# Combine weights turned by VectorE and DMAs instead of TensorE, in the second expert mixture

## The chip, the cores and the metric

The kernel runs on one core of one Trainium2 chip, as one launch. The metric is the time of that launch on the device in microseconds. The core has TensorE (matmuls, with a weight load PEld that overlaps them), VectorE (DVE), ScalarE (ACT), GpSimd (POOL) and SyncE (SP), whose queue issues the DMAs.

## The reference

Three stages follow one another: an attention with a memory, a soft mixture of experts, and a second mixture whose weights are balanced by eight rounds of normalisation. The change touches only the third.

```python
def _moe_ref(x, phi, w1, w2):
    ...
    c = logits - logits.max(1, keepdims=True)
    c = np.exp(c)
    c /= c.sum(1, keepdims=True) + 1e-09
    return (c @ slot_out).astype(np.float32)      # [2304, 32] @ [32, 512]

def _moe2_ref(x, w_gate, w1, w2):                 # N = 2304, D = 512, E = 8, F = 1024
    logits = x @ w_gate
    logits = logits - logits.max()
    P = np.exp(logits)
    for _ in range(8):
        P /= P.sum(1, keepdims=True) + 1e-09
        P /= P.sum(0, keepdims=True) + 1e-09
        P *= N / E
    out = np.zeros((N, D), dtype=np.float32)
    for e in range(E):
        h = np.maximum(x @ w1[e], 0.0)
        ye = h @ w2[e]
        out += P[:, e:e + 1] * ye
    return out.astype(np.float32)
```

## The kernel before, in words

The input x of the second mixture is c @ slot_out, with only 32 slots. So the kernel doesn't form x. For each expert it multiplies the 32 slot rows with w1 once (`prepare_a`, line 1092, the slots' product `pa`), splits the result into a high and a low part (`split_a`) and spreads both by DMAs into a tile `a4` of 128 rows (`move_a`, line 1125). The first layer is then `layer1` (line 1145): a matmul of `a4` with `c4T`, which holds c transposed, 128 rows by 2304 tokens: two copies of the rounded c and two of its remainder, 32 rows each. The product of the four row blocks gives the full precision. As relu commutes with a positive factor, the expert's weight P[:, e] is folded into c. So `c4T` must be made anew for each expert.

Making it (lines 1313 to 1338) is done in pieces of two units by three steps. `scale_c`: VectorE multiplies c by the weight (`cP`), ScalarE rounds it (`chi`) and writes it twice into `c4`, VectorE writes the remainder twice. `turn_c`: TensorE transposes each tile of 128 tokens into PSUM (`pc`, line 1331). `store_c`: ScalarE copies the result to `c4T` (line 1336). Pieces of an expert come at units 6 to 9 and, for the last unit's two tiles (the leftovers), at unit 10, counted from the start of the expert before; `c_steps` puts the three steps behind products 1, 2 and 3 of the unit.

The work is cut into units: 8 experts by 9 units of 256 tokens. A unit's second layer is a product of 2 x 2 blocks in seven block products (`PRODS`, in the `ORDER` p5, p1, p7, p6, p2, p3, p4), numbered k = 0 to 6. Each is 12 matmuls of 128 x 256: over four row blocks f, high by high (line 1451), high by low (1452), low by high (1453). After product 1 of unit g comes `layer1` of unit g + 1, eight matmuls. So a unit is 84 + 8 = 92 matmuls. The first five units of expert 0 use a plain product instead.

Around the products, `hidden` makes the seven left operands of the next unit from PSUM: ScalarE rounds (line 1175) and VectorE (1169, 1182) and GpSimd (1186) make sums and remainders. `collect` adds finished products into the accumulators (1467). The weights of the next expert are summed and split by `w_sum` (1045), `w_hi` (1048, ScalarE) and `w_lo` (1054, GpSimd, one of them VectorE) in the same way. The late blocks B11, T3, B21 and B22 (tiles `BB1`, `BB2`) are shared by all experts, so they are rounded only in the last unit of the expert before and the first of the new one, just behind their last use.

The order is written out by hand: `beside(s, f, ...)` appends a step to slot s = 7 g + k, `at(u, k, ...)` is slot 7 u + k, and in each slot the program emits the product, then `hidden` and `collect`, then what `beside` left there. Each engine runs its own instructions in that order; they wait for each other by semaphores. SP issues its DMAs in the same program order but runs ahead of the other engines until one of its own waits stops it: the loads of w1 and w2 wait for the tiles' last readers, `move_a` for `split_a`. The buffer `ps_a` in PSUM, one bank, serves `pc` and `pa` in turn.

One earlier DMA is of use below: `load_memory` (line 174) moves, in the first stage, 64 partitions x 4 pairs of heads x 65 numbers of 4 bytes.

Of the kernel before, what the change touches and what calls it, by code (L numbers as in the profile page):

```python
# [8 lines left out]
F32 = mybir.dt.float32  # L9
# [12 lines left out]
def infini_attention_soft_moe_sinkhorn_moe(  # L22
# [22 lines left out]
    P = 128  # L45
# [1006 lines left out]
    def w_lo(e, nm, i, g):  # L1052
# [9 lines left out]
    Cw = mD.tile([P, NTT, NS], F32, name="Cw")  # L1062
    sel = mD.tile([P, 4, 160], F32R, name="sel")
    nc.vector.tensor_scalar(
        out=sel.rearrange("p j c -> p (j c)"), in0=ones[:, 0:1].to_broadcast([P, 640]),
        scalar1=0.0, scalar2=None, op0=ALU.mult,
# [157 lines left out]
    m2 = mS.tile([1, 1], F32, name="m2")  # L1224

    def gate_slots():
        soB = G["soB"] = mB.tile([P, KD, 4, NS], F32, tag="c4", name="soB")
        nc.scalar.activation(out=soB, in_=soR.to_broadcast([P, KD, 4, NS]), func=AF.Copy)
# [84 lines left out]
    def scale_c(e, u0, u1):  # L1313
        T0, n = 2 * u0, 2 * (u1 - u0)
        cP = mB.tile([P, 4, NS], F32, tag="cP", name="cP")[:, 0:n]
        nc.vector.tensor_tensor(
            out=cP, in0=Cw[:, T0 : T0 + n], in1=Pr[:, T0 : T0 + n, e : e + 1].to_broadcast([P, n, NS]),
            op=ALU.mult,
        )
        chi = mB.tile([P, 4, NS], F32R, tag="chi", name="chi")[:, 0:n]  # L1320
        nc.scalar.activation(out=chi, in_=cP, func=AF.Copy)
        c4 = cs_[e, u0] = mB.tile([P, 4, 4, NS], F32, tag="c4", name="c4")
        hb = chi.bitcast(F32).rearrange("p t (o s) -> p t o s", o=1).to_broadcast([P, n, 2, NS])
        cb = cP.rearrange("p t (o s) -> p t o s", o=1).to_broadcast([P, n, 2, NS])
        nc.scalar.activation(out=c4[:, 0:n, 0:2, :], in_=hb, func=AF.Copy)
        nc.vector.tensor_tensor(out=c4[:, 0:n, 2:4, :], in0=cb, in1=hb, op=ALU.subtract)
# [8 lines left out]
    def store_c(e, u0, u1):  # L1335
        nc.scalar.activation(
            out=c4T[:, UT * u0 : UT * u1], in_=G["pc"][:, 0 : UT * (u1 - u0)], func=AF.Copy
        )


    side = {}
# [27 lines left out]

    def c_steps(v, e, u0, u1):  # L1370
        at(v, 1, scale_c, e, u0, u1)
        at(v, 2, turn_c, e, u0, u1)
        at(v, 3, store_c, e, u0, u1)

# [14 lines left out]
    for e in range(1, E):  # L1389
        v = NU * (e - 1)  # L1390
        for i in range(5):
            c_steps(v + 6 + i, e, 2 * i, min(2 * i + 2, NU))
        at(v, 0, load_w1, e, e % 2)
# [3 lines left out]
        at(v + 1, 4 + (e == 1), split_a, e)  # L1397
        at(v + 1, 5 + (e == 1), move_a, e)
        for i in range(2):
# [6 lines left out]
            at(v + 6 + i, 2, w_sum, e, "T3", i, "P")  # L1406
        for nm, k in (("B11", 2), ("T3", 4), ("B21", 6), ("B22", 8)):
            for i in range(2):
                at(v + 8, k + i, w_hi, e, nm, i)
                at(v + 8, k + i + (nm[0] == "B" and nm[1] == "2"), w_lo, e, nm, i, "D" if nm == "B22" and i else "P")  # L1410
# [30 lines left out]
    def product(g, k):  # L1441
        e, u = units[g]
        a, b = PRODS[ORDER[k]]
        bank, half = PLACE[ORDER[k]]
        if (g, bank) not in Y:
            Y[g, bank] = ps_y.tile([P, DM], F32, tag="y", name=bank)
        o_ = Y[g, bank][:, CW * half : CW * half + CW]
        hh, hl = X[g, a, "h"], X[g, a, "l"]
        wh, wl = W[e, b, "h"], W[e, b, "l"]
        for f in range(KH):  # L1450
            nc.tensor.matmul(o_, hh[:, f, :], wh[:, f, :], start=f == 0, stop=False)  # L1451
            nc.tensor.matmul(o_, hh[:, f, :], wl[:, f, :], start=False, stop=False)  # L1452
            nc.tensor.matmul(o_, hl[:, f, :], wh[:, f, :], start=False, stop=f == KH - 1)  # L1453
        return o_
# [197 lines left out]
```

## Time and profile before

| | us |
|---|---|
| median of 3 runs | 1119.05 |
| the runs | 1119.82, 1119.05, 1113.94 |
| the profiled execution | 1122.88 |
| its span | 1120.9 |

The second mixture fills the profile from about 300 us to the end. TensorE is busy for 97% of the span, so a time is best read from the distance between the starts of its instructions, not from their durations: a 128x256 matmul is shown with 0.28 us, and the next one starts 0.11 us later. DVE is busy for 74%, POOL for 63%, ACT for 58%.

### The profile page before, as it was taken

The numbers are of one execution on the slowest core, as the hardware profiler recorded it, in microseconds if no ns is written. First come the engines' busy times: TensorE is split into PE (matmuls) and PEld (weight loads), VectorE is DVE, ScalarE is ACT, GpSimd is POOL, SyncE is SP. The second block draws the span as 40 slices with busy tenths as digits, with TensorE's granted clock in tenths as the row PEclk, the third lists the DMA queues.
The fourth block names the chain that finished last, engine by engine and source line by source line (L and its number), as shares of the span: only waits on it lengthen the run. The fifth ranks groups of instructions, "written<-read, shape, count | busy, mean of one in ns | idle before, by whom it ended". The sixth has DMA issues, their size and how long they took to land.

```text
span 1120.9 us, 24593 instructions
## 1 busy us (share of the span) xinstructions
PE 1085.3 (97%) x9269; PEld 996.0 (89%) x9269; DVE 830.7 (74%) x1813; ACT 645.4 (58%) x1392; POOL 703.7 (63%) x634
## 2 busy tenths in 40 slices
PE   6999999989999999999999999999999999999998
PEld 4887878763577899999999999999999999999998
DVE  7888888753266467788778778877977777788775
ACT  7988989741343675556455545644564555456442
POOL 6655556300252777688577768866776676778665
PEclk8999999988899999999999999999999999999999
DMA  9476767578702013004101300310030022000111
GB/s 208 127 215 188 222 183 216 152 290 346 313 22 73 1 54 107 12 1 142 29 1 39 118 16 1 113 58 1 11 142 20 1 102 69 1 2 20 44 53 58
DMA packets 42646, 105.73 MB, mean 94 GB/s; under 512 B 8224, under 2 KB 18592, under 8 KB 38432
## 3 DMA queue, kind: packets, MB, share of 16 engines
q1 hardware_dynamic: 42096, 104.07, 28.6%
q8 instruction: 74, 1.21, 0.4%
q14 instruction: 44, 0.36, 0.1%
q10 hardware_dynamic: 432, 0.09, 0.0%
HBM read 95.74 MB, written 4.72 MB: 90 GB/s over the span
## 4 chain that ended last, share of the span: by engine, by line
PE 80%; DVE 6%; ACT 5%; DMA 4%; issue 4%; POOL 1%; SPq 0%; DVEq 0%; ACTq 0%; POOLq 0%
PE y L1451 19%; PE y L1452 19%; PE y L1453 19%; PE l L1145 6%; PE po L476 3%; PE pt L437 2%; ACT sm L394 2%; PE y L1418 2%; DMA wm<-in_moe_w_dram 2%; PE pa L1092 1%; PE pc L1331 1%; DMA w<-in_moe_w_dram 1%; PE ps L371 1%; PE ps L366 1%; DVE sm L387 1%
## 5 line engine op out<-in xcount | busy, mean ns | idle before, releaser
L1169 DVE SCALAR_TENSOR_TENSOR f<-l,f 128x512 f32<-128x512 f32 x268 | 184.2, 687 | 59.7 <-ACT a11h L1175 49.8
L1186 POOL TENSOR_TENSOR s1l<-f,s1h 128x512 fp32r<-128x512 f32 x67 | 90.3, 1347 | 155.2 <-ACT s1h L1175 155.2
L1467 DVE TENSOR_TENSOR accA<-accA,y 128x512 f32<-128x512 f32 x125 | 85.5, 684 | 48.6 <-PE y L1453 48.3
L1175 ACT ACTIVATE a12h<-l 128x512 fp32r<-128x512 f32 x72 | 43.2, 600 | 101.8 <-PE y L1453 95.0
L1186 POOL TENSOR_TENSOR s4l<-f,s4h 128x512 fp32r<-128x512 f32 x67 | 87.4, 1304 | 15.7 <-PE y L1452 10.3
L1467 DVE TENSOR_TENSOR accB<-accB,y 128x512 f32<-128x512 f32 x125 | 85.7, 686 | 7.5
L1186 POOL TENSOR_TENSOR s3l<-f,s3h 128x512 fp32r<-128x512 f32 x67 | 87.1, 1299 | 0.0
L1186 POOL TENSOR_TENSOR s2l<-f,s2h 128x512 fp32r<-128x512 f32 x67 | 86.9, 1298 | 0.0
L1165 ACT ACTIVATE f<-l 128x512 f32<-128x512 f32 x67 | 39.7, 592 | 76.1 <-PE l L1145 72.9
L1145 PE MATMUL l<-c4T,a 128*128 128x256 f32 x576 | 80.4, 283 | 2.2 <-DVE a22l L1182 2.2
L1054 POOL TENSOR_TENSOR BB1l<-raw,BB1h 128x512 fp32r<-128x512 f32 x32 | 41.3, 1304 | 63.3 <-ACT BB1h L1048 63.3
L1451 PE MATMUL y<-T2h,s2h 128*128 128x256 f32 x268 | 77.7, 290 | 0.0
L1145 PEld LDWEIGHTS l<-c4T,a 128*128 128x128 f32 x576 | 73.2, 191 | 4.1 <-DVE a22l L1182 3.7
L394 ACT ACTIVATE sm<-sm,mn 128x128 f32<-128x128 f32 (+3 forms) x128 | 70.9, 556 | 8.0 <-DVE mn L387 7.6
L1451 PE MATMUL y<-BB2h,a12h 128*128 128x256 f32 x268 | 75.1, 280 | 0.0
L1451 PE MATMUL y<-BB1h,s3h 128*128 128x256 f32 x268 | 75.0, 280 | 0.0
L1453 PE MATMUL y<-BB1h,s3l 128*128 128x256 f32 x268 | 75.0, 280 | 0.0
L1452 PE MATMUL y<-BB1l,s3h 128*128 128x256 f32 x268 | 75.0, 280 | 0.0
L1452 PE MATMUL y<-BB2l,s4h 128*128 128x256 f32 x268 | 74.8, 279 | 0.0
L1452 PE MATMUL y<-T2l,s2h 128*128 128x256 f32 x268 | 74.7, 279 | 0.0
L1453 PE MATMUL y<-T2h,s2l 128*128 128x256 f32 x268 | 74.7, 279 | 0.0
L1451 PE MATMUL y<-BB2h,s4h 128*128 128x256 f32 x268 | 74.6, 278 | 0.0
(315 smaller groups left out, 4211.3 us busy)
## 6 DMA issues: line engine op xcount, KB each, us to landing
wm<-in_moe_w_dram SPq DMA_DIRECT2D x32, 1024.0 KB, 7.5
raw<-in_moe_w_dram SPq DMA_DIRECT2D x32, 512.0 KB, 4.2
w<-in_moe_w_dram SPq DMA_DIRECT2D x32, 512.0 KB, 4.3
qd<-in_q_dram SPq DMA_DIRECT2D x30, 288.0 KB, 4.3
kd<-in_k_dram SPq DMA_DIRECT2D x30, 288.0 KB, 4.6
qp<-in_q_dram SPq DMA_DIRECT2D x15, 288.0 KB, 2.9
vt<-in_v_dram SPq DMA_DIRECT2D x16, 256.0 KB, 4.6
out_dram<-accB SPq DMA_DIRECT2D x18, 128.0 KB, 1.8
```

Source lines behind the costliest of these rows:

```text
L394: nc.scalar.activation(out=sm[:, 0:n], in_=sm[:, 0:n], func=AF.Exp, scale=-1.0, bias=mnc, accum_out=X.sums[:, i, h : h + 1],)
L476: nc.tensor.matmul(po[64 * h : 64 * h + 64, c0:w], X.vt[:, j, h, :], rhs, start=(j == 0), stop=(j == n - 1),)
L1054: eng(g).tensor_tensor(out=w_tile(e, nm, "l")[:, h], in0=full(e, nm, i), in1=w_tile(e, nm, "h")[:, h].bitcast(F32), op=ALU.subtract,)
L1145: nc.tensor.matmul(ph[:, f, :], a4s[e][:, P * (KH * j + f) : P * (KH * j + f) + P], c4T[:, UT * u : UT * u + UT], start=True, stop=True,)
L1165: nc.scalar.activation(out=f_tile(g, nm), in_=ph(g, nm), func=AF.Relu)
L1169: nc.vector.scalar_tensor_tensor(out=f_tile(g, nm), in0=ph(g, src), scalar=0.0, in1=b, op0=ALU.max, op1=op)
L1175: nc.scalar.activation(out=h_tile(g, nm, "h"), in_=ph(g, nm) if a else FU[g, nm], func=AF.Relu if a else AF.Copy)
L1186: nc.gpsimd.tensor_tensor(out=lo, in0=FU[g, nm], in1=hi, op=ALU.subtract)
L1451: nc.tensor.matmul(o_, hh[:, f, :], wh[:, f, :], start=f == 0, stop=False)
L1452: nc.tensor.matmul(o_, hh[:, f, :], wl[:, f, :], start=False, stop=False)
L1453: nc.tensor.matmul(o_, hl[:, f, :], wh[:, f, :], start=False, stop=f == KH - 1)
L1467: nc.vector.tensor_tensor(out=acc, in0=acc, in1=y, op=ALU.add)
```

## The change

In `sel` and in `gate_slots`, tiles get other names and sizes so that they can be shared; nothing else is done with them. The rest, in the order of the diff:

- Sixteen of an expert's eighteen token tiles are turned in two rounds of eight (`c_round` and the list in the loop over experts). `part_c`: GpSimd multiplies c by the weight, 128 x 256. `round_c`: ScalarE rounds it. `blocks_c`: VectorE transposes it, in blocks of 32 x 32, first the rounded part (z = 0), later the remainder (z = 1), which `rest_c` makes on GpSimd. `move_c`: SP moves the blocks to their rows and columns of `c4T`, 16 DMAs a round, each 32 partitions x 8 tiles x 32 numbers.
- Round 0 starts in unit 4 (unit 5 for expert 1), product 2, of the expert before; round 1 runs in unit 1 of the expert itself, products 0 to 4. The two leftover tiles keep `scale_c`, `turn_c` and `store_c` in unit 1, products 1 to 3, ahead of `prepare_a` of the next expert.
- `move_a` goes from unit 1, product 5, to unit 3.
- The late blocks are rounded one product sooner.
- In the first unit of an expert, a product with a late block takes its high by low terms behind all the others.

```diff
+        if e:
+            cw = mB.tile([P, 2, CW], F32, tag="ft", name="cf").rearrange("p a c -> p (a c)")
+        else:
+            cw = cw_tile()
...
+    NR = 8
+    WR = NR * NS
...
+    def part_c(e, r):
+        cw = ct_[e, r] = cw_tile()
+        nc.gpsimd.tensor_tensor(
+            out=cw[:, 0:WR].rearrange("p (t s) -> p t s", s=NS), in0=Cw[:, NR * r : NR * r + NR],
+            in1=Pr[:, NR * r : NR * r + NR, e : e + 1].to_broadcast([P, NR, NS]), op=ALU.mult,
+        )
+
+    def round_c(e, r):
+        cw = ct_[e, r]
+        nc.scalar.activation(
+            out=cw[:, WR : 2 * WR].bitcast(F32R), in_=cw[:, 0:WR], func=AF.Copy
+        )
+
+    def rest_c(e, r):
+        cw = ct_[e, r]
+        nc.gpsimd.tensor_tensor(
+            out=cw[:, 0:WR], in0=cw[:, 0:WR], in1=cw[:, WR : 2 * WR], op=ALU.subtract
+        )
+
+    def blocks_c(e, r, z):
+        if z == 0:
+            ct_[e, r, "t"] = mD.tile([P, 640], F32, tag="sel", name="ct")
+        cw = ct_[e, r]
+        nc.vector.transpose(
+            ct_[e, r, "t"][:, WR * z : WR * z + WR], cw[:, WR * (1 - z) : WR * (2 - z)]
+        )
+
+    def move_c(e, r, zs):
+        ct = ct_[e, r, "t"]
+        to = c4T[:, 0:N].bitcast(F32).rearrange("p (t j n) -> p t j n", j=4, n=32)
+        for z in zs:
+            for j in range(4):
+                nc.sync.dma_start(
+                    to[32 * z : 32 * z + 32, NR * r : NR * r + NR, j],
+                    ct[32 * j : 32 * j + 32, WR * (z // 2) : WR * (z // 2) + WR].rearrange(
+                        "p (t n) -> p t n", n=32
+                    ),
+                )
...
-    def c_steps(v, e, u0, u1):
-        at(v, 1, scale_c, e, u0, u1)
-        at(v, 2, turn_c, e, u0, u1)
-        at(v, 3, store_c, e, u0, u1)
+    def c_round(s, e, r):
+        for k, f, *a in (
+            (0, part_c), (1, round_c), (2, blocks_c, 0), (5, rest_c), (6, blocks_c, 1),
+        ):
+            beside(s + k, f, e, r, *a)
+        beside(s + 3, move_c, e, r, (0, 1))
+        beside(s + 7, move_c, e, r, (2, 3))
...
-        for i in range(5):
-            c_steps(v + 6 + i, e, 2 * i, min(2 * i + 2, NU))
+        c_round(7 * (v + 4 + (e == 1)) + 2, e, 0)
+        for k, f, *a in (
+            (0, part_c), (1, round_c), (2, blocks_c, 0), (2, rest_c), (3, blocks_c, 1),
+            (3, move_c, (0, 1)), (4, move_c, (2, 3)),
+        ):
+            at(v + 10, k, f, e, 1, *a)
+        at(v + 10, 1, scale_c, e, NU - 1, NU)
+        at(v + 10, 2, turn_c, e, NU - 1, NU)
+        at(v + 10, 3, store_c, e, NU - 1, NU)
...
-        at(v + 1, 5 + (e == 1), move_a, e)
+        at(v + 3, 3 * (e == 1), move_a, e)
...
-        for nm, k in (("B11", 2), ("T3", 4), ("B21", 6), ("B22", 8)):
+        for nm, k in (("B11", 1), ("T3", 3), ("B21", 5), ("B22", 7)):
...
-        for f in range(KH):
-            nc.tensor.matmul(o_, hh[:, f, :], wh[:, f, :], start=f == 0, stop=False)
-            nc.tensor.matmul(o_, hh[:, f, :], wl[:, f, :], start=False, stop=False)
-            nc.tensor.matmul(o_, hl[:, f, :], wh[:, f, :], start=False, stop=f == KH - 1)
+        terms = ((hh, wh), (hh, wl), (hl, wh))
+        seq = [(f, t) for f in range(KH) for t in terms]
+        if u == 0 and e and (b[0] == "B" or b == "T3"):
+            seq = [(f, t) for f in range(KH) for t in terms[::2]] + [(f, terms[1]) for f in range(KH)]
+        for n, (f, (a, b)) in enumerate(seq):
+            nc.tensor.matmul(o_, a[:, f, :], b[:, f, :], start=n == 0, stop=n == 3 * KH - 1)
```

## Rows read from the trace of the kernel before

**Rows 1.** The page's busy us, share of the span and instructions of each engine.
```profile
PE 1085.3 (97%) x9269; PEld 996.0 (89%) x9269; DVE 830.7 (74%) x1813; ACT 645.4 (58%) x1392; POOL 703.7 (63%) x634
```

**Rows 2.** Windows of one unit: length, busy us (instructions) of PE, PEld, DVE, ACT, POOL; clock; DMA.
```profile
449.68:460.11 10.43, 10.43 (x94) 10.43 (x94) 8.03 (x14) 5.55 (x10) 7.26 (x6) 1.00 0.10 24
491.39:502.28 10.89, 10.89 (x98) 10.89 (x98) 9.96 (x16) 6.09 (x12) 8.66 (x8) 1.00 0.01 2
513.33:524.52 11.19, 11.19 (x99) 11.19 (x98) 8.49 (x15) 8.44 (x16) 8.96 (x8) 1.00 0.63 236
647.82:658.65 10.83, 10.83 (x94) 10.83 (x94) 7.98 (x13) 5.12 (x9) 7.57 (x6) 1.00 0.10 23
```

**Rows 3.** Chain that ended last, in order of time: start us, length us, engine, tile.
```profile
391.82 0.91 PE l L1145 x8
...
638.68 1.87 PE pa L1092 x32
647.82 0.94 PE l L1145 x8
658.65 0.94 PE l L1145 x8
...
691.16 0.94 PE l L1145 x8
...
1099.83 0.94 PE l L1145 x8
```

**Rows 4.** Groups from 380 us: xcount | busy us, mean ns | idle before, releaser.
```profile
L1331 PE MATMUL pc<-ident,c 128*128 128x128 f32 x126 | 19.6, 273 | 0.0
...
L1316 DVE TENSOR_TENSOR cP<-Cw,Pr 128x128 f32<-128x128 f32 x28 | 18.7, 668 | 0.0
...
L1326 DVE TENSOR_TENSOR c<-cP,chi 128x256 f32<-128x256 f32 x28 | 24.1, 860 | 12.1 <-ACT chi L1321 12.1
...
L1365 POOL TENSOR_TENSOR accD<-accD,accA 128x256 f32<-128x256 f32 x9 | 7.2, 799 | 5.2 <-DVE accA L1467 5.2
...
L1467 DVE TENSOR_TENSOR accD<-accD,y 128x256 f32<-128x256 f32 x125 | 52.0, 416 | 4.3 <-PE y L1453 1.4
```

**Rows 5.** Waits of PE and PEld from 380 us: total us, times, longest us.
```profile
PEld l L1145 <- DVE a22l L1182: 1.4, 7, 0.4
PEld pa L1092 <- ACT c4T L1336: 1.1, 3, 0.6
PE pa L1092 <- ACT c4T L1336: 0.4, 1, 0.4
PE l L1145 <- DVE a22l L1182: 0.2, 1, 0.2
```

**Rows 6.** Timeline of PE across four transposes: start us, length us, instruction.
```profile
603.25 0.60 PE L1331 MATMUL pc<-ident,c 128*128 128x128 f32 x4
603.61 0.36 PE L1451 MATMUL y<-T2h,s2h 128*128 128x256 f32 x1
```

**Rows 7.** Timeline of DVE and POOL, units 0 and 1 of expert 3.
```profile
627.75 1.46 DVE L1054 TENSOR_TENSOR BB2l<-raw,BB2h 128x512 fp32r<-128x512 f32 x1
...
628.61 1.76 POOL L1186 TENSOR_TENSOR s1l<-f,s1h 128x512 fp32r<-128x512 f32 x1
...
632.89 1.30 POOL L1186 TENSOR_TENSOR s4l<-f,s4h 128x512 fp32r<-128x512 f32 x1
638.38 1.28 POOL L1186 TENSOR_TENSOR s1l<-f,s1h 128x512 fp32r<-128x512 f32 x1 [4.18 <-ACT s1h L1175]
```

**Rows 8.** DMAs of move_a (line 1125): issue on SP in ns, min/median/max; landing.
```profile
L1125 SPq DMA_DIRECT2D a<-ahi x56: 507/588/596, 333.8 to 948.8; - x56
L1125 SPq DMA_DIRECT2D a<-alo x56: 534/589/1825, 336.4 to 951.4; - x56
...
DMA to landing us min/median/max: 1.8/1.8/3.8
```

**Rows 9.** DMAs of load_memory (line 174): issue on SP in ns, min/median/max.
```profile
L174 SPq DMA_DIRECT2D mbd<-in_M_prev_dram x8: 548/576/610, 7.5 to 177.9; - x8
```

More of the change, by code (lines that the diff above doesn't have):

```diff
@@ L1062, in infini_attention_soft_moe_sinkhorn_moe @@
     Cw = mD.tile([P, NTT, NS], F32, name="Cw")
-    sel = mD.tile([P, 4, 160], F32R, name="sel")
+    sel0 = mD.tile([P, 640], F32, tag="sel", name="sel").bitcast(F32R)
+    sel = sel0.rearrange("p (j c) -> p j c", j=4)
     nc.vector.tensor_scalar(
-        out=sel.rearrange("p j c -> p (j c)"), in0=ones[:, 0:1].to_broadcast([P, 640]),
+        out=sel0, in0=ones[:, 0:1].to_broadcast([P, 640]),
         scalar1=0.0, scalar2=None, op0=ALU.mult,
@@ L1224, in infini_attention_soft_moe_sinkhorn_moe, with cw_tile @@
     m2 = mS.tile([1, 1], F32, name="m2")
+    def cw_tile():
+        return mB.tile([P, 768], F32, tag="cw", name="cw")
     def gate_slots():
-        soB = G["soB"] = mB.tile([P, KD, 4, NS], F32, tag="c4", name="soB")
+        soB = G["soB"] = cw_tile()[:, 0:512].rearrange("p (c a s) -> p c a s", c=KD, a=4)
         nc.scalar.activation(out=soB, in_=soR.to_broadcast([P, KD, 4, NS]), func=AF.Copy)
@@ L1314, in scale_c @@
         T0, n = 2 * u0, 2 * (u1 - u0)
-        cP = mB.tile([P, 4, NS], F32, tag="cP", name="cP")[:, 0:n]
+        if e:
+            cw = mB.tile([P, 2, CW], F32, tag="ft", name="cf").rearrange("p a c -> p (a c)")
+        else:
+            cw = cw_tile()
+        o_ = 4 * NS * (2 if e else 4)
+        w = n * NS
+        cP = cw[:, o_ : o_ + w].rearrange("p (t s) -> p t s", s=NS)
         nc.vector.tensor_tensor(
@@ L1319, in scale_c @@
         )
[L1320 to L1323, printed above, removed]
+        chi = cw[:, o_ + w : o_ + 2 * w].rearrange("p (t s) -> p t s", s=NS)
+        nc.scalar.activation(out=chi.bitcast(F32R), in_=cP, func=AF.Copy)
+        c4 = cs_[e, u0] = cw[:, 0:o_].rearrange("p (t a s) -> p t a s", a=4, s=NS)
+        hb = chi.rearrange("p t (o s) -> p t o s", o=1).to_broadcast([P, n, 2, NS])
         cb = cP.rearrange("p t (o s) -> p t o s", o=1).to_broadcast([P, n, 2, NS])
@@ L1338, in store_c @@
         )
+    NR = 8
+    WR = NR * NS
+    ct_ = {}
+    def part_c(e, r):
[32 more added lines that the diff above has]
+                )
     side = {}
```

## The prediction

> **What bounds the kernel now.** I first read the busy shares [rows 1]: TensorE is busy for 1085.3 us of a span of 1120.9, VectorE, ScalarE and GpSimd 58 to 74%. So the second mixture is limited by the number of matmuls and by what separates two of them; another engine counts only where TensorE waits for it. Then I read single units from the windows [rows 2]. A unit without side work takes 10.43 us for its 92 matmuls (84 of the products, 8 of layer1), 0.113 us each. A unit in which four blocks of c are turned takes 10.89. But there is a third kind: a unit of the same 92 matmuls and no transposes takes 10.83, at the same granted clock (1.00, the 2.4 GHz level), TensorE busy throughout: 0.118 us a matmul. So the stream runs at one of two paces, and the pace holds over many units: between two layer1 groups of one expert, 647.82 to 691.16, four units take 43.34 us, 10.84 each [rows 3]. What sets the pace the trace doesn't name. I see only that it can change at an interruption of the stream (four transposes, the slots' product, a wait) and that no unit without one changed it. The unit of 11.19 [rows 2] is one that began with four transposes and then ran at the slow pace.
>
> The chain of waits gives the balance [rows 3]. From the layer1 group at 391.82 to the one at 1099.83 there are 64 unit lengths: 708.0 us, where 64 × 10.43 = 667.5 would be the floor, so 40.5 us are lost. 28 groups of four transposes (126 transposes in all are 28 × 4 + 7 × 2 [rows 4]) at 0.46 (10.89 − 10.43) take 12.9. The 7 leftover pairs take half, 1.6. The slots' product six times at 1.87 [rows 3] and 0.1 of restart, as behind the transposes, takes 11.8. TensorE's waits for ScalarE and VectorE are 1.4 + 0.2 + 1.1 + 0.4 = 3.1 [rows 5]. What is left, 11.1 us, is the slow pace: of the 64 × 0.40 = 25.6 that it would cost if it always held, some 43%.
>
> **The change part by part.** (1) 112 of the 126 transposes leave TensorE, with their 28 interruptions: −12.9 us. The instruction row alone misleads here: one transpose lasts 273 ns [rows 4], yet the next product starts 0.36 us after the first of four [rows 6], because they are pipelined; the rest of the 0.46 is the restart. The Trainium skill ("TensorE: Matmul & The Clock Gate", section "Part 4: PE-mode transpose") gives about 275 ns for a transpose within a kernel; if each cost the stream that, the sum would be an estimated −31 us instead of −12.9. The duration in the trace agrees with the page, the distance between starts does not, and the units' lengths decide.
>
> (2) VectorE loses, per expert, four times cP (0.67) and the remainder (0.86, with a wait for ScalarE in between) and gains four 128x256 block transposes. The trace shows none. The nearest rows are 128x256 VectorE operations: 0.42 for one that reads PSUM, 0.86 on average for one that reads SBUF only [rows 4]; the slowest 128x512 one beside a busy GpSimd took 1.46 [rows 7]. I take 0.42 to 0.86, ends 0.42 and 1.46. In the steady units VectorE is busy 8.03 of 10.43 us [rows 2], which covers even the upper end; without that cover 28 × 1.46 would be 41 us. Price: 0.
>
> (3) ScalarE loses four c4T copies of 128x512 per expert and more small ones, and gains two roundings of 128x256. Price: 0, it is idle for half of each unit [rows 2].
>
> (4) GpSimd gains four 128x256 operations per expert. The nearest row is accD at 0.80 [rows 4]; bounds half of a 128x512 one, 0.65, and the longest s1l, 1.76 [rows 7]. GpSimd is busy 7.26 of 10.43 [rows 2], so 0.8 fits into the unit; in unit 1 of an expert it stands idle from 634.19 to 638.38 [rows 7], where part_c and rest_c of round 1 fall. New is the wait: round_c on ScalarE waits for GpSimd; behind it stand chi of the leftover pair, the relu copies of the next unit, and behind those turn_c and prepare_a on TensorE. Price 0 as long as GpSimd is through with s4l by about 634.2, as it is before.
>
> (5) 32 DMAs per expert on SP, each of 256 pieces of 128 B. They go in front of nothing that is late: move_a of the next expert moves two units back and is needed five units after that, and the w1 loads come at the expert's end. One move_a DMA of 32 pieces takes 0.59 us of the queue and lands 1.8 us after issue [rows 8]; one of the memory's DMAs, also 256 pieces (64 partitions × 4 pairs of heads, 260 B each), takes 0.58 [rows 9]. So the 16 DMAs of a round take 16 × 0.62 = 9.9 us, with 0.03 between two. Round 1 has the nearer deadline: in the expert whose slots' product starts at 638.68 (that is one product behind the turning step) the fifth unit's layer1 starts at 658.65 [rows 3]; with the first blocks turned at about 639.1 there are 19.5 us; the last DMA lands about 9.9 + 1.3 = 11.2 us after the first is issued (1.3 is what the landing lasts beyond the issue). 8 us are spare: price 0.
>
> (6) Late blocks. The rounding of the four late weight blocks starts one product earlier, VectorE's share of it (BB2l, 1.46 [rows 7]) follows no c work any more, and in unit 0 the terms that read the low weights come last. This goes against VectorE's lateness, for which TensorE waits at layer1 (1.6 us in all [rows 5]). But TensorE also reaches that place 0.46 us sooner. I take −1.0 of 1.6, bounds −1.6 and +1. The wait of the slots' product for c4T (1.5 us [rows 5]) stays: turn_c, store_c and prepare_a keep their order.
>
> (7) The pace. Before, 35 interruptions by transposes and six by the slots' product drew it anew; after, seven boundaries do, and each draw holds for nine units, 9 × 0.40 = 3.6 us. I see no reason for a better or a worse draw: 0, bounds −11.1 (always fast) and +14.5 (always slow).
>
> Sum on the profiled execution: it took 1122.88 us (span 1120.9 and 2.0 around it), −12.9 − 1.0 gives 1109.0. The median of the runs is 1119.05, 3.8 below the profiled one: about one nine-unit stretch at the other pace (the runs spread from 1113.94 to 1119.82). From the median the sum is 1105.2. I take the middle, 1107.
>
> **The rivals.** *DMAs late* (slower). If a DMA with 128 B pieces held SP's queue or its landing much longer, layer1 of the fifth unit waits in every expert. The point is (19.5 − 1.3) / 16 = 1.14 us per DMA. At 1.83, the longest move_a issue [rows 8], the round ends 16 × 1.83 + 1.3 = 30.6 us after its start, 11.1 too late, 7 times: 78 us, so 1185. For it: each has 256 pieces, eight times the 32 of a move_a DMA. Against it: the 256-piece row took 0.58. The Trainium skill ("DMA: Bandwidth & Descriptors", section "Specifications") asks for at least 512 B per transfer for full rate, below which the engine reads, modifies and writes; that speaks for this rival, and the trace of before has no piece of 128 B within SBUF to test it. Chance 0.06.
>
> *The pace falls badly.* After the leftover pair and the slots' product every expert runs slow: 1109 + 14.5 = 1123.5, no change. For it: the units from 647.82 ran slow after exactly these two events [rows 3]; against it: the one from 449.68 ran at 10.43 after the same ones [rows 2]. Chance 0.06. *The pace falls well*: 1109 − 11.1 = 1098. Chance 0.10.
>
> *A new wait in unit 1.* If GpSimd is late or its product of c takes 1.76, ScalarE stands in round_c by about 1.0 to 1.4 us more, and TensorE at the leftover pair or the slots' product: 7 × 1.3 = 9.1, so 1116, within 0.5% of before. For it: GpSimd runs without a gap from the late blocks to 634.19 [rows 7]. Against it: those blocks begin one product sooner. Chance 0.08.
>
> **How the numbers follow.** The forecast has the remaining 0.70, with a range of its own of 1102 to 1113 (waits −1.6 to +1, two stretches of 3.6 either way less what the median levels out). A measurement of this kernel can tell about 0.5% from no change, here 5.6 us: faster means under 1113.5, slower over 1124.6. Faster: 0.10 and all but 0.02 of the 0.70, 0.78. Same: 0.02, 0.06 and 0.08, 0.16. Slower: 0.06. The range takes in the good pace and the forecast, 1097 to 1115, and leaves out the other three.
>
> **What would show it.** Right: 14 transposes in the profile instead of 126; steady units of 10.43 or 10.84 with nothing between, units 4, 5 and 1 included; VectorE's wait at layer1 shorter; DMAs of c near 0.6 us each on SP, and layer1 of the fifth unit not waiting for any. Wrong: TensorE waiting for c4T's DMAs, for ScalarE's c4T copy by more than before, or for VectorE's low parts in units 4 and 5; or a count of slow-pace units far from 43%, which would move the time by 0.40 us each with every step above right.

## The result, and the profile after

The changed kernel took 1102.99 us (median of 4 runs, 1100.15 to 1108.35), the kernel before, beside it on the same chip, 1116.75 (4 runs, 1113.94 to 1119.82): a ratio of 0.988, interval 0.9848 to 0.9912, or 13.8 us. Two later sessions gave 0.9799 (0.9773 to 0.9825) and 0.9823 (0.9789 to 0.9857), that is 20.2 and 18.9 us. The forecast was 1107.0 and its range 1097 to 1115. The profiled execution took 1105.7 us with a span of 1103.9.

The page of the changed kernel, engines as in [rows 1]:

```profile
PE 1066.3 (97%) x9157; PEld 978.4 (89%) x9157; DVE 804.6 (73%) x1785; ACT 620.9 (56%) x1322; POOL 719.7 (65%) x662
```

TensorE has 112 instructions fewer, exactly the transposes. Next its windows, columns as in [rows 2]. The first runs from layer1 of unit 7 to layer1 of unit 71, which is the stretch that the prediction balanced; then come a unit in which blocks of c are turned, a plain unit, a unit 1 (with the slots' product), and one that stands out:

```profile
386.44:1082.64 696.20, 693.07 (x6096) 686.10 (x6095) 530.25 (x883) 361.64 (x659) 534.30 (x437) 1.00 0.21 57
...
580.42:590.85 10.43, 10.43 (x95) 10.43 (x94) 8.00 (x14) 5.16 (x9) 8.78 (x8) 1.00 0.01 2
645.96:656.79 10.83, 10.83 (x94) 10.83 (x93) 7.97 (x13) 5.11 (x9) 7.57 (x7) 1.00 0.04 10
907.26:919.82 12.56, 10.87 (x94) 10.70 (x93) 10.77 (x14) 4.77 (x9) 9.84 (x9) 1.00 0.26 90
...
622.03:635.12 13.09, 13.09 (x128) 12.04 (x127) 9.73 (x18) 6.11 (x13) 7.09 (x6) 1.00 0.23 34
```

The stretch lasts 696.2 us; before it was 708.0 [rows 3], so 11.8 of the gain lie in it. The two profiled spans differ by 17.0 because the changed execution also came to the stretch 5.2 us sooner (386.44 against 391.66 in the two traces). I don't credit that to the change: over all versions of it that I ran, which have nearly the same work ahead of that point, the point lay anywhere from 385.8 to 390.9. It goes with the granted clock, which ahead of it stood at 0.50 (the 1.2 GHz level) for 34 us in the trace of before, for 20 us in that of the changed kernel, and again for 34 us in the version that came there at 390.9.

In the chain of the changed kernel (columns as in [rows 3]) an expert now holds one pace from its unit 1 on:

```profile
626.16 1.86 PE pa L1093 x32
635.29 0.94 PE l L1146 x8
646.12 0.94 PE l L1146 x8
...
721.97 0.94 PE l L1146 x8
...
734.82 0.91 PE l L1146 x8
745.25 0.91 PE l L1146 x8
```

From 635.29 to 721.97 eight units take 86.68 us, 10.84 each; from 734.82 on the next expert has 10.43. Of the seven experts here the third, fifth and seventh ran slow, the others fast. The groups that answer to [rows 4], with the new operations (columns as there):

```profile
L1378 DVE STREAM_TRANSPOSE ct<-cw 128x256 f32<-128x256 f32 x27 | 11.8, 436 | 3.3 <-POOL cw L1370 3.2
L1054 DVE TENSOR_TENSOR BB2l<-raw,BB2h 128x512 fp32r<-128x512 f32 x7 | 11.0, 1570 | 0.0
L1370 POOL TENSOR_TENSOR cw<-cw 128x256 f32<-128x256 f32 x14 | 10.4, 744 | 3.7 <-ACT cw L1364 3.7
L1357 POOL TENSOR_TENSOR cw<-Cw,Pr 128x256 f32<-128x256 f32 x13 | 8.3, 641 | 0.0
...
L1364 ACT ACTIVATE cw<-cw 128x256 fp32r<-128x256 f32 x13 | 5.3, 411 | 11.2 <-POOL cw L1357 11.2
...
L1341 PE MATMUL pc<-ident,cf 128*128 128x128 f32 x14 | 2.7, 274 | 1.0 <-ACT f L1166 1.0
```

The waits of PE and PEld in the changed kernel (columns as in [rows 5]):

```profile
PE y L1518 <- DVE accD L1532: 1.7, 1, 1.7
PE pc L1341 <- ACT f L1166: 1.0, 1, 1.0
PE y L1518 <- ACT accD L1530: 0.4, 1, 0.4
...
PEld y L1518 <- issue: 4.3, 7, 1.9
PEld pc L1341 <- ACT f L1166: 1.1, 1, 1.1
PEld y L1518 <- ACT accD L1530: 0.6, 1, 0.6
PEld pa L1093 <- ACT c4T L1346: 0.3, 1, 0.3
```

Layer1 waits for VectorE no more, and the slots' product hardly for c4T. But two single waits of 1.7 and 1.0 us are new, and a small one of 0.4. A wait stands in both lists, on PEld some 0.2 us longer, so each counts once, by PEld: 1.9 + 1.1 + 0.6 + 0.3 = 3.9 us now, 1.4 + 1.1 = 2.5 before [rows 5] (the other six issue waits, 0.4 each behind the slots' product, stand in the trace of before too). The balance of the stretch closes: 667.5 as the floor, 1.6 for the pairs, 6 × (1.86 + 0.1) = 11.8 for the slots' product, 3.9 of waits, and 10.8 for 2405 slow matmuls, those in the stretch that the next one follows after 116 to 120 ns (some 117.8 instead of 113.3, so 4.5 each); that is 695.6 of 696.2. Against the balance before, the transposes are gone and the rest has hardly moved.

Below, a stretch **without the pace** is its length less that excess of its slow matmuls: 697.6 before (2319 of them, 10.4 us), 685.4 after. Two more traces of the changed kernel, told below, gave 686.3 and 683.7, so one trace against another says nothing below some 2.5 us. (The expectations below name 2559 and 1096 slow matmuls for two of the three, by a count that is a little wider and runs on to the end of the program; here they are 2405 and 1085.)

### The profile page after: what moved, and what is told of

The parts are those of the page before. It is cut to its first block, busy times and chain, and to the rows that moved or that the text cites. A ratio compares the mean times of both kernels' runs of the same rounds, so it can differ in the third digit from the quotient of the medians.

```text
span 1103.9 us, 24598 instructions
## 1 busy us (share of the span) xinstructions
PE 1066.3 (97%) x9157; PEld 978.4 (89%) x9157; DVE 804.6 (73%) x1785; ACT 620.9 (56%) x1322; POOL 719.7 (65%) x662
## 4 chain that ended last, share of the span: by engine, by line
PE 74%; POOL 5%; DVE 5%; issue 5%; ACT 5%; DMA 5%; SPq 0%; DVEq 0%; ACTq 0%; POOLq 0%
PE y L1518 53%; PE l L1146 5%; PE po L476 3%; PE pt L437 2%; DMA kd<-in_k_dram 2%; ACT sm L394 2%; DMA wm<-in_moe_w_dram 1%; PE pa L1093 1%; DMA w<-in_moe_w_dram 1%; POOL BB2l L1054 1%; PE y L1481 1%; PE ps L371 1%; PE ps L366 1%; DVE sm L387 1%; PE ph L890 1%
## 5 line engine op out<-in xcount | busy, mean ns | idle before, releaser
L1187 POOL TENSOR_TENSOR s1l<-f,s1h 128x512 fp32r<-128x512 f32 x67 | 87.2, 1301 | 128.7 <-ACT s1h L1176 119.6
L1518 PE MATMUL y<-T2h,s2h 128*128 128x256 f32 x268 | 75.2, 280 | 0.0
L1518 PE MATMUL y<-T4h,a22h 128*128 128x256 f32 x268 | 74.5, 278 | 0.0
L1518 PE MATMUL y<-T4l,a22h 128*128 128x256 f32 x268 | 74.5, 278 | 0.0
L1518 PE MATMUL y<-T4h,a22l 128*128 128x256 f32 x268 | 74.5, 278 | 0.0
L1518 PE MATMUL y<-T1h,s1h 128*128 128x256 f32 x268 | 74.5, 278 | 0.0
L1518 PE MATMUL y<-T1l,s1h 128*128 128x256 f32 x268 | 74.5, 278 | 0.0
```

The costliest lines, as they stand in the source:

```text
L1187: nc.gpsimd.tensor_tensor(out=lo, in0=FU[g, nm], in1=hi, op=ALU.subtract)
L1518: nc.tensor.matmul(o_, a[:, f, :], b[:, f, :], start=n == 0, stop=n == 3 * KH - 1)
```

## The experiments

**Do the transposes cost 0.46 us a group?** Into the changed kernel I put 28 groups of four transposes whose result nobody reads, where the kernel before had its own. Theory: the price is TensorE's, and comes back whole. Rival: part of the gain is relief of the other engines.

```diff
+    def idle_turns():
+        pd = aux("pd")
+        for t in range(4):
+            nc.tensor.transpose(pd[:, P * t : P * t + P], ident, ident)
...
+        for i in range(4):
+            at(v + 6 + i, 2, idle_turns)
```

> The changed kernel with four transposes of the identity, read by nobody, behind product 2 of each unit in which the kernel before turned four blocks (28 groups). Nothing else waits for them. Theory A (the interruption of TensorE's stream is the price, not what VectorE and ScalarE did for the transposes): the stretch grows by 28 x 0.46 = 12.9 us to about 709, ratio to the kernel before about 1.0. Rival B (the gain comes from freed VectorE and ScalarE): it grows by the 0.36 us that four transposes last or less, hidden in part, to 700 to 703, ratio 0.990 to 0.994. Also open: the pace behind each group. If a group draws the pace anew, slow units stand after some of them also in experts that ran fast, and odd experts turn fast behind some.

Measured: 1105.38 us, 0.9918 of before (0.989 to 0.9947). Three windows, a plain unit and two with a group (columns as in [rows 2]):

```profile
452.53:462.95 10.42, 10.42 (x94) 10.42 (x93) 8.03 (x14) 5.55 (x10) 7.58 (x7) 1.00 0.08 18
483.81:494.69 10.88, 10.88 (x98) 10.88 (x97) 7.99 (x13) 5.12 (x9) 9.23 (x9) 1.00 0.01 2
494.69:505.58 10.89, 10.89 (x99) 10.89 (x98) 7.99 (x13) 5.61 (x10) 7.59 (x7) 1.00 0.03 6
```

Each of the 28 units with a group takes 10.88 or 10.89, 0.46 more than a plain one, so step (1)'s price holds. Yet the stretch was 695.1, below both forecasts and no longer than the changed kernel's: only 173 of its matmuls were slow (0.8 us instead of 10.8), and the waits were all but gone (0.5 on PEld instead of 3.9). Without the pace it is 694.3 against 685.4, 8.9 more: 12.9 for the groups less some 4 of waits and short pauses that they hid.

**Which part of the change gains?** One kernel has the new way of turning c but the old late rounding and the old order of terms; the other is the kernel before with only the late rounding moved and the terms in the new order.

```diff
-        for nm, k in (("B11", 1), ("T3", 3), ("B21", 5), ("B22", 7)):
+        for nm, k in (("B11", 2), ("T3", 4), ("B21", 6), ("B22", 8)):
...
-        if u == 0 and e and (b[0] == "B" or b == "T3"):
-            seq = [(f, t) for f in range(KH) for t in terms[::2]] + [(f, terms[1]) for f in range(KH)]
```

> The changed kernel with the late blocks rounded at their old places and with the old order of terms; only the turning of c and the place of move_a differ from before. Measure: the stretch from the layer1 of unit 7 to that of unit 71, which took 708.0 us in the kernel before and 696.2 in the changed one. Theory A (the gain is TensorE's: 28 groups of four transposes at 0.46 us, 12.9 in all; the waits give nothing): about 696, ratio about 0.988 as for the whole change, give or take one stretch at the other pace (3.6 us). Rival B (a good part of the gain is waits that the earlier rounding and the order of terms take away, at least 3 us): 699 or more, ratio 0.992 or more. Rival C (the earlier rounding costs: VectorE's late block took 3.4 us once and TensorE stood for 1.9 us): 694, and no wait of more than 0.7 us of TensorE in the first unit of an expert.

> The kernel before with the late blocks rounded one product sooner and the high by low terms last in an expert's first unit; c is turned by TensorE as before. Theory A: the 126 transposes stay and with them the time: 708 us in the stretch, within 3.6; ratio 0.997 to 1.003. Rival B (the waits are the gain): 705 or less, with TensorE's waits for VectorE at layer1 (1.6 us before) and for the late blocks gone; ratio 0.997 or less. Rival C (the earlier rounding costs): 709 to 711, ratio above 1.001.

Turning alone: 1108.47 us, 0.9944 (0.9918 to 0.997), a stretch of 698.7. Rounding alone: 1118.69, 1.003 (1.001 to 1.0051), a stretch of 709.5, so no gain: the wait for VectorE at layer1 is gone, but PEld waits 3.2 us in all for VectorE's accD in the units 0 instead. The waits of PEld and PE in the kernel with turning alone, then its unit 0 of one expert and the unit before it (columns as in [rows 5] and [rows 2]):

```profile
PE y L1516 <- POOL BB2l L1054: 4.8, 7, 0.7
...
PEld y L1516 <- POOL BB2l L1054: 7.6, 13, 0.9
```

```profile
620.76:632.72 11.96, 11.19 (x95) 10.79 (x93) 9.57 (x16) 5.28 (x10) 11.87 (x10) 1.00 0.43 133
610.33:620.76 10.43, 10.43 (x95) 10.43 (x93) 7.84 (x13) 8.17 (x15) 8.03 (x7) 1.00 0.68 248
```

In unit 0 GpSimd is busy for 11.87 of 11.96 us: without the transposes the low halves of the late blocks are what TensorE waits for, in every expert. Is it the work on c, new on GpSimd, that makes them late? The first operation of GpSimd's row of late blocks in this expert, with turning alone and in the kernel before (start, length, and the idle time ahead of it):

```profile
612.73 1.30 POOL L1054 TENSOR_TENSOR BB1l<-raw,BB1h 128x512 fp32r<-128x512 f32 x1 [3.16 <-ACT BB1h L1048]
614.59 1.29 POOL L1054 TENSOR_TENSOR BB1l<-raw,BB1h 128x512 fp32r<-128x512 f32 x1 [3.73 <-ACT BB1h L1048]
```

No: GpSimd stood idle ahead of the row in both, and it starts 2.4 us behind layer1 in both (610.33 and 612.17). Without the pace the stretch is 691.7 (1558 slow matmuls): turning alone gains 5.9 of the 12.2, the earlier rounding and the order of terms the other 6.3, which on the kernel before are worth nothing (698.4 against 697.6). Which of these two is worth how much, no run separates.

**Do the DMAs have the room that the sum gave them?** Each DMA of c was split in two of half the tiles, so the pieces are the same and the DMAs twice as many.

```diff
-            for j in range(4):
+            for j, h in ((j, h) for j in range(4) for h in (0, 4)):
+                c0 = WR * (z // 2) + 32 * h
                 nc.sync.dma_start(
-                    to[32 * z : 32 * z + 32, NR * r : NR * r + NR, j],
-                    ct[32 * j : 32 * j + 32, WR * (z // 2) : WR * (z // 2) + WR].rearrange(
-                        "p (t n) -> p t n", n=32
-                    ),
+                    to[32 * z : 32 * z + 32, NR * r + h : NR * r + h + 4, j],
+                    ct[32 * j : 32 * j + 32, c0 : c0 + 128].rearrange("p (t n) -> p t n", n=32),
```

> The changed kernel with each DMA of c split in two of four tiles: 64 DMAs per expert and 128 pieces each, the same bytes. If the queue's price goes by the DMA (0.61 us each), round 1 takes 32 x 0.64 = 20.5 us instead of 10.3, from about 625 to 646 in the expert whose fifth unit's layer1 started at 646.0. Theory A (the moves are hidden with some 9 us to spare, and the point is 1.14 us per DMA of old size): just past it, waits of 0 to 2 us at the layer1 of the fifth unit in each expert, 0 to 14 us in all, stretch 696 to 710, and the moves of round 0 hidden as before. Rival (the price goes by the pieces, 256 of them taking 0.61 us): nothing changes, 696, each DMA near 0.3 us. Third (SP delays the loads of the weights by it): TensorE waits at the slots' product or GpSimd for raw tiles.

Measured: 1128.47 us, 1.0124 (1.0092 to 1.0155). The DMAs of c in the changed kernel (issue and landing as in [rows 8]), and a round of them on SP's timeline (start, length):

```profile
L1387 SPq DMA_DIRECT2D c4T<-ct x224: 585/609/1687, 379.9 to 1031.1; - x112
...
DMA to landing us min/median/max: 1.9/2.0/3.6
```

```profile
625.07 10.88 SPq L1387 DMA_DIRECT2D c4T<-ct  x16
```

The same two of the split kernel, and its wait of PE:

```profile
L1388 SPq DMA_DIRECT2D c4T<-ct x448: 585/599/1884, 379.9 to 1060.9; - x150
```

```profile
638.46 22.89 SPq L1388 DMA_DIRECT2D c4T<-ct  x32
```

```profile
PE l L1146 <- DMA c4T<-ct: 20.2, 7, 4.0
```

A DMA of 128 pieces holds SP for 599 ns, one of 256 for 609: the price goes by the DMA. Whole, a round is issued in 10.88 us and landed at 637.28, 8.7 before layer1 of the fifth unit at 645.96; split, its 22.89 us are too long, and that layer1 waits once in each of the seven experts, 2.9 us on average. The stretch is 720.1, 10 us more than the expectation allowed: the waits come to 20.2 instead of 14 at most, and behind the four longest of them, 3.0 to 4.0 us, the granted clock fell to 0.50 (the 1.2 GHz level), for 20 us in all, which costs some 8.6 us more in all in the unit behind each. Behind the three waits of 2.0 to 2.3 us it stayed at 1.00. One of the four units (columns as in [rows 2]):

```profile
557.06:570.52 13.46, 13.46 (x93) 13.46 (x93) 7.39 (x12) 5.22 (x9) 7.95 (x7) 0.79 0.17 40
```

So *DMAs late* was a real rival with its point about where the sum had put it, and the price of one DMA decided against it. The Trainium skill ("DMA: Bandwidth & Descriptors", section "Why small descriptors are slow (HBM only)") exempts transfers within SBUF from the penalty for small pieces; these 128 B pieces agree, at 0.61 us a DMA and 2.0 to its landing against 0.59 and 1.8 for `move_a` [rows 8], which moves as many bytes.

**What sets the pace?** Where a stream turned slow, the second matmul of product 5 had come some 150 ns after the first instead of 113, and I took GpSimd's `s4l`, which this product reads, for the cause. So its late terms were put further back:

```diff
-            seq = [(f, t) for f in range(KH) for t in terms[::2]] + [(f, terms[1]) for f in range(KH)]
+            seq = [(f, t) for t in (terms[0], terms[2], terms[1]) for f in range(KH)]
```

> The changed kernel; only the order of an expert's first products with a late block differs: high by high for all four row blocks, then low by high, then high by low (before: high by high and low by high in turns). In the changed kernel's trace TensorE stands for 0.04 us at the second matmul of product 5 of the first unit, where it needs the low part of s4; behind this wait the stream runs at 117.8 ns a matmul, and behind the leftover pair and the slots' product that follow it the whole expert does. Theory A (the pace of an expert is set by this small wait at its start): without it the stream reaches the pair at 113.3, and every expert runs at 113.3 behind the slots' product: the stretch from layer1 of unit 7 to unit 71 falls from 696.2 to 685 to 688, under 500 slow matmuls instead of 2559, ratio to the kernel before 0.977 to 0.981. Rival B (the pace falls anew at each boundary, whatever came before): about as many slow experts as before, 3 or 4 of 8; 692 to 699. Rival C (the pace goes by the expert, odd ones slow): 696.

Measured: 1100.71 us, 0.9824 (0.9799 to 0.9849), a stretch of 690.9 instead of 685 to 688, and 1613 slow matmuls. The short gap stood where it had been, though the second matmul no longer reads `s4l`: this cause is refuted. Next, the pair of leftovers was taken off TensorE (nine tiles a round), one idle group of four transposes was put into unit 0 of each expert, and the changed kernel was run again as it is:

```diff
-    NR = 8
+    NR = 9
...
-        at(v + 10, 1, scale_c, e, NU - 1, NU)
-        at(v + 10, 2, turn_c, e, NU - 1, NU)
-        at(v + 10, 3, store_c, e, NU - 1, NU)
```

> The changed kernel with nine tiles in each round, so that no leftover pair is turned on TensorE. Removed: 7 pairs (0.14 us and a restart of 0.1 each), ScalarE's and VectorE's work on them in unit 1, and the slots' product's wait for the c4T copy (0.09 us in most experts, 0.24 in one). Theory A (as for the transposes): -7 x 0.3 = 2.1 us and the pair's wait of 1.1 us in the last expert, 693 in the stretch at the same share of slow units; the moves take 16 DMAs of 288 pieces, still hidden. Rival B (the pair is what turns the stream to the pace behind the slots' product): other experts are slow than in the changed kernel, 3.6 us for each, 684 if none, 710 if all. Rival C (a wait for ScalarE's rounding of 288 columns or for the moves): layer1 of the fifth unit waits.

```diff
+        at(v + 9, 2, idle_turns)
```

> The changed kernel with one group of four idle transposes of the identity behind product 2 of each expert's first unit (7 groups). With four such groups per expert every unit behind the slots' product ran at 113.3 ns a matmul. Theory A (the last group, in the first unit, delays TensorE by 0.46 us, and with this the small wait at product 5 goes): as with four groups, no slow expert; cost 7 x 0.46 = 3.2, gain 11.3 and the waits: stretch 683 to 688. Rival B (the groups in units 6 to 8 did it): the slow experts stay, 696 + 3.2 = 699. Rival C (the odd experts are slow for another reason): 699 too, with the same experts slow.

> The changed kernel itself once more, beside the others on the same chip. If the pace follows from the small wait in an expert's first unit, the same experts (3, 5 and 7) are slow as in its first trace, and the stretch takes 696 within 1; if it falls anew in each execution, other experts are slow and the stretch lies anywhere between 688 and 707. Ratio to the kernel before 0.985 to 0.991.

Nine tiles: 1107.58 us, 0.9889 (0.9865 to 0.9913); a stretch of 694.3 with 3224 slow matmuls, 14.5 us. Without the pace it is 679.8, the shortest of all: it saves the pairs and TensorE's waits, and the pace takes that back. One idle group: 1100.62, 0.9828 (0.9807 to 0.9849); 638 slow matmuls, all experts fast except the last. Its stretch is 692.7 all the same, above the 683 to 688 expected: in unit 0 of the first expert a single wait of 1.9 us for accD came (the first kind of the two below), the granted clock fell to 0.50 behind it, and that unit took 14.65 us instead of 10.89. The changed kernel again: 1099.65, 0.9799 (0.9773 to 0.9825), better than the 0.985 to 0.991 expected, a stretch of 691.2; in its profiled run only the fourth expert ran slow, 1085 matmuls, where in the first trace three had. So the draw of the pace is not fixed by the program. But the program may weigh it: on the same chip the four runs with nine tiles took 1104.5 to 1110.3 us, the five of the changed kernel 1094.3 to 1100.5, though without the pace nine tiles are the shorter by 6 us.

**The two new waits.** The first one, in the sixth expert. The timelines of VectorE, GpSimd and TensorE of the changed kernel there (start, length, engine, operation):

```profile
909.81 3.41 DVE L1054 TENSOR_TENSOR BB2l<-raw,BB2h 128x512 fp32r<-128x512 f32 x1
913.14 0.68 DVE L1170 SCALAR_TENSOR_TENSOR f<-l,f 128x512 f32<-128x512 f32 x1
913.75 0.41 DVE L1532 TENSOR_TENSOR accD<-accD,y 128x256 f32<-128x256 f32 x1
```

```profile
908.87 2.56 POOL L1054 TENSOR_TENSOR BB2l<-raw,BB2h 128x512 fp32r<-128x512 f32 x2
911.36 1.31 POOL L1187 TENSOR_TENSOR s1l<-f,s1h 128x512 fp32r<-128x512 f32 x1
914.62 1.30 POOL L1187 TENSOR_TENSOR s2l<-f,s2h 128x512 fp32r<-128x512 f32 x1 [1.95 <-ACT s2h L1176]
```

```profile
914.30 0.36 PE L1518 MATMUL y<-BB2h,s4h 128*128 128x256 f32 x1 [1.69 <-DVE accD L1532]
```

VectorE's BB2l, 0.92 to 1.34 us elsewhere in this trace, took 3.41 and ended at 913.22, 0.55 after GpSimd's last operation of an unbroken row (911.36 + 1.31 = 912.67). It stands ahead of accD, whose collection frees the bank that product 5 writes, so TensorE stood for 1.69. The second wait, in the last expert, on GpSimd and ScalarE:

```profile
1014.32 1.33 POOL L1415 TENSOR_TENSOR accB<-accB,accA 128x512 f32<-128x512 f32 x1
1015.57 0.78 POOL L1418 TENSOR_TENSOR accD<-accD,accA 128x256 f32<-128x256 f32 x1
1016.26 1.33 POOL L1187 TENSOR_TENSOR s4l<-f,s4h 128x512 fp32r<-128x512 f32 x1
1017.54 0.65 POOL L1357 TENSOR_TENSOR cw<-Cw,Pr 128x256 f32<-128x256 f32 x1
```

```profile
1018.22 0.42 ACT L1364 ACTIVATE cw<-cw 128x256 fp32r<-128x256 f32 x1 [3.33 <-POOL cw L1357]
```

The output's closing sums stand ahead of `part_c`, so `round_c` waits 3.33 us, and the relu copy and the pair behind it are late by 1.0. One kernel puts VectorE's BB2l one slot later, behind accD; a second one also moves the closing sums of the last expert's unit 0 to product 4 of unit 1; a third has both and the idle group of unit 0; with it the changed kernel ran once more.

```diff
-                at(v + 8, k + i + (nm[0] == "B" and nm[1] == "2"), w_lo, e, nm, i, "D" if nm == "B22" and i else "P")
+                at(v + 8, k + i + (nm[0] == "B" and nm[1] == "2") + (nm == "B22" and i), w_lo, e, nm, i, "D" if nm == "B22" and i else "P")
```

> The changed kernel with VectorE's part of the late rounding (the low half of B22) one product later, behind the collecting of product 2 (accD). In two traces of the changed kernel TensorE's product 5 of an expert's first unit waits for that accD operation: 0.04 us in most experts and 1.85 and 2.5 where the rounding in front of it took 3.4 and 3.8 us beside GpSimd instead of 1.34. Theory A (that wait is the one that sets the pace of the expert behind it): it is gone, every expert runs at 113.3 ns a matmul except the last, where GpSimd's closing sums hold up the leftover pair; under 900 slow matmuls (1096 and 2559 in the two traces), stretch 684 to 689. Rival B (the low half of B22 is now late for the high by low terms of product 5, which start about 0.9 us behind its first matmul): a wait there instead, 0.2 us or more per expert, slow experts as before, 691 or more. Rival C (the pace does not depend on this wait): 691 to 697 with no wait of product 5.

```diff
-                    add_u(u, "PP")
-                    send(0, 1, B_[:, 0:CW])
-                    send(1, 1, B_[:, CW:])
-                send(1, 0, D_)
+
+                    def close():
+                        add_u(u, "PP")
+                        send(0, 1, B_[:, 0:CW])
+                        send(1, 1, B_[:, CW:])
+                        send(1, 0, D_)
+
+                    at(g + 1, 4, close) if u == 0 else close()
+                else:
+                    send(1, 0, D_)
```

> As the one before, and in the last expert GpSimd's closing sums of unit 0 (accB and accD with accA, 2.1 us) with their three output DMAs come at product 4 of unit 1 instead of ahead of its low part of s4 and of part_c. In the changed kernel ScalarE stood for 3.3 us there in round_c, and TensorE 1.1 to 1.5 us at the leftover pair. Theory A: that wait goes, 1.1 to 1.5 us less than the kernel without this step, and the last expert runs at 113.3 too (up to 2 us in the stretch, 3 us to the end): stretch 682 to 686, no slow expert. Rival B (the sums hold up something else of GpSimd in unit 1 or 2): a wait of TensorE for s2 or s3 in unit 2 of the last expert.

> This is the version with the two waits taken out (the low half of B22 one slot later on VectorE, the last expert's closing sums behind part_c) and in addition one idle group of four transposes in unit 0 of each expert, as the run with one idle group had it: 0.46 us each. Theory (the group brings the stream to the fast pace at each expert's start, and it stays there): experts' steady units at 10.43, unit 0 at 10.89, unit 1 at 12.78, in all seven experts but for the last, and no VectorE BB2l over 2 us. From the fast experts of the version without the group the stretch from layer1 of unit 7 to unit 71 is then 683.5 + 7 x 0.46 = 686.7 us, and the median about 1096. Rival (the group does nothing for the pace, the fast experts of the earlier run were a lucky draw): two or three of the seven experts at 10.84, the stretch 690 to 697, the median 1099 to 1105, above the version without the group by the 3.2 us that the groups cost.

> The changed kernel as it is, on the same chip as the version above, so that the two stand beside the same runs of the kernel before. Ratio to before 0.980 to 0.988 as in its two earlier rounds, median 1099 to 1104; the experts that run slow are others than in the first two traces if the draw of the pace is by chance, and the same (the 2nd, 4th and 6th pair of boundaries) if the order of the instructions fixes it. Against the version with both waits taken out and the idle groups it should be 3 to 8 us slower if that theory holds, and within 2 us of it if the rival does.

| kernel | median us | ratio (interval) | stretch | slow matmuls | without the pace |
|---|---|---|---|---|---|
| BB2l behind accD | 1104.75 | 0.9899 (0.9865 to 0.9933) | 693.6 | 2263 | 683.4 |
| and closing sums later | 1098.88 | 0.9862 (0.9827 to 0.9896) | 689.5 | 1470 | 682.9 |
| and idle groups | 1100.20 | 0.9827 (0.9787 to 0.9868) | 692.9 | 983 | 688.4 |
| the changed kernel | 1100.40 | 0.9823 (0.9789 to 0.9857) | 691.4 | 1700 | 683.7 |

The first two took out what they were made for: every unit 0 of the experts took just its pace, 10.43 or 10.84, without the small wait for accD, and the last expert's unit 1 went from 11.63 to 11.06 at the same pace. The long BB2l itself came in neither; but it didn't come in the last row's trace either, the changed kernel as it is, so that shows nothing. Against the three traces of the changed kernel, 683.7 to 686.3, what is gained is too little to be seen, in the medians too. And the small wait is not what sets the pace: without it three experts and two ran slow, 693.6 and 689.5 us where 684 to 689 and 682 to 686 were expected. The third was expected at 1096 if the idle group fixes the pace. The pace came out so: from its unit 2 on every expert ran fast but the last. But the long BB2l came back, twice, though it stands behind accD now (VectorE and GpSimd of that kernel, and the two units 0, columns as above and in [rows 2]):

```profile
522.71 3.96 DVE L1054 TENSOR_TENSOR BB2l<-raw,BB2h 128x512 fp32r<-128x512 f32 x1
```

```profile
523.57 1.31 POOL L1187 TENSOR_TENSOR s1l<-f,s1h 128x512 fp32r<-128x512 f32 x1
524.82 1.31 POOL L1187 TENSOR_TENSOR s2l<-f,s2h 128x512 fp32r<-128x512 f32 x1
528.10 1.29 POOL L1187 TENSOR_TENSOR s3l<-f,s3h 128x512 fp32r<-128x512 f32 x1 [1.98 <-ACT s3h L1176]
```

```profile
420.24:432.75 12.51, 11.90 (x99) 11.33 (x97) 10.10 (x15) 5.09 (x9) 9.57 (x9) 1.00 0.28 93
519.05:531.96 12.91, 11.58 (x99) 11.02 (x97) 11.14 (x15) 4.71 (x8) 9.97 (x9) 1.00 0.28 91
```

Again it ended 0.54 us after GpSimd's row (526.67 against 526.13), and TensorE, waiting for BB2l and then for layer1's a22l, stood for 1.9 us in these two units, which took 12.51 and 12.91 us where the other units 0 with a group took 10.89. With the seven groups at 0.46 that ate up the good pace: 1100.20 us, as the rival had it, and within 0.2 of the changed kernel beside it. So no version here beats the changed kernel by more than its spread.

## Why the prediction was right, and where it was not

The mechanism and the time were right: 13.8 us by the medians, 11.8 by the stretch, 13.9 forecast in the steps. That the medians meet the steps within 0.1 is luck of the draw: the later sessions gave 20.2 and 18.9 us, the stretches of the three traces lie 11.8, 16.8 and 16.6 below the one trace of before, and without the pace 12.2, 11.3 and 13.9. The forecast balance had counted two waits twice (0.4 and 0.2 us of PE lie within 1.1 and 1.4 of PEld), which leaves 11.7 for the pace where the slow matmuls come to 10.4.

(1) Right in size: 28 groups at 0.46 are what the idle groups brought back. What the step did not say is that on its own it gains only half: the kernel with the turning alone lost 6 of the 12 us, and waited for GpSimd's low halves in every expert.

(2), (3) Right: VectorE's block transpose took 0.436 us, near the lower end taken; all of it is hidden.

(4) The operations took 0.64 and 0.74 us against 0.80 taken. The wait of `round_c` that I had called a rival came in every expert, 1.1 to 1.4 us in six and 3.3 in the last, but TensorE was late by it in the last one alone, where the closing sums stand ahead of s4l and `part_c`: 1.0 us instead of 9.1.

(5) Right, and tested from the other side: 0.61 us a DMA against 0.62, 8.7 us spare against 8.

(6) This is the step that failed, by its size and by its place. I costed the earlier rounding at −1.0 of a wait for VectorE at layer1, as a part that stands by itself. That wait did go, but two single ones came, and the sum of waits rose by 1.4 (2.5 to 3.9). The part's true worth, with the order of the terms, is some 6 us, and only together with (1): it holds back a wait for GpSimd that the transposes had covered. I had not asked, of the stall removed in (1), what is late next in unit 0; the sum came out because the change brings the answer with it. The two misses cancel in the total: nothing was charged to (1), nearly nothing credited to (6).

(7) No change was forecast, and 2405 slow matmuls against 2319 are none. But that is one execution: three traces of the same changed kernel had 2405, 1085 and 1700. At 4.5 ns each these are 5.9 us between two executions, half of the gain in the stretch. They stay within the two stretches of 3.6 us either way that I had allowed.

## What to carry to other kernels

Of each stall removed ask what stands next behind it in that very stage, and whether the same change takes care of it: two edits that gain nothing alone or half alone can be one gain together. A DMA on a queue costs by the DMA, so the time by which a round of them is landed can be summed up beforehand from one row of the same queue, if it is a row of a like DMA: the loads of the weights take 0.33 us on it, these 0.6. And where a stream has two paces, read what a step costs from what is left without the pace, but choose a kernel by many executions: nine tiles were the shortest without the pace and the slowest of the four kernels with the new turning that ran on that chip.

## What the runs showed of the hardware

**Two paces of the matmul stream.** At a granted clock of 1.00 (2.4 GHz) the 128x256 matmuls start every 113.3 or every 117.8 ns, and keep to it over a whole expert of nine units. With an idle group of four transposes in unit 0 twelve of 14 experts in two kernels ran fast, the last one slow in both; without it one to three of seven ran slow in the traces of the changed kernel. These are few draws: that a group changes the draw fits them, but is not shown, and why there are two paces stays open.

**The clock behind a wait.** In the stretch the granted clock left 1.00 only behind waits of TensorE for a DMA or for VectorE: behind five of them, one of 1.9 us with the one idle group and four of 3.0 to 4.0 in the split kernel, it fell to 0.50 (the 1.2 GHz level) for a while; behind five others, of 1.7 to 2.3 us, it stayed at 1.00.

**VectorE beside GpSimd.** VectorE's BB2l reads two operands from SBUF. In most cases it started within one GpSimd operation and ended some 0.55 us after the next had begun, which then took about 1.75 us instead of 1.31, as s1l did before [rows 7]. In five cases, of seven in each of 14 traces, it took 3.1 to 4.0 us, and each time ended 0.54 or 0.55 after the third GpSimd operation, counted from the one it started within, with which the row ended (3.41 and 3.96 above). So one of the two stands while the other works. The Trainium skill ("SBUF — State Buffer", section "SBUF: two separate sides") states it as an exclusive lock on a shared pair of ports, held for the whole instruction; the trace agrees, and adds that VectorE can be passed over at two changes in a row. What decides that is open: the start is not it, 0.3 to 0.9 us before the end of GpSimd's operation in usual cases and 0.06 to 0.9 in long ones.
